# Scale and shift of the first norm folded into the query, key and value weights by another way, in a transformer block on one Trainium2 core

## The chip, the cores and the metric

One core of one Trainium2 chip. The metric is device time in microseconds for one launch. The kernel before takes 413.95 us, the median of three runs (413.38 to 415.32). A profiled execution of it took 416.01 us.

## What is computed

A block with adaptive layer norm: six modulation vectors come from a condition `c`; a linear attention with softmax feature maps; a feed-forward part with relu. x is 2048 x 576 in bf16, 32 heads of 18, feed-forward width 4608.

```python
mod = (silu(c) @ w_mod).reshape(1, 6, 1, 576)
sa, ca, ga, sb, cb, gb = ...                     # the six parts of mod
h = layernorm(x) * (1 + ca) + sa
q, k, v = split(h @ wqkv)                        # 32 heads of 18
pq, pk = q @ w_phi, k @ w_phi                    # per head
phi_q = concat(softmax(pq), softmax(-pq))        # 36 features; phi_k alike from pk
kv, z = phi_k^T v, sum over tokens of phi_k
o = (phi_q kv) / (phi_q z + 1e-6)
x = x + ga * (o @ wo)
h = layernorm(x) * (1 + cb) + sb
out = x + gb * (relu(h @ w1) @ w2)
```

## The kernel before

Tokens are in 16 tiles of 128 (t); two tiles are a unit or pair (u, p, n), four a block (b). The 576 features are five chunks of up to 128 (ci; the last has 64). The order of the work is one list of steps, written out by hand (line 922), that fixes the order on TensorE (PE), VectorE (DVE), ScalarE (ACT) and the DMA queue that SyncE (SP) issues; a step puts its instructions on the engines that it uses. An argument of 1 at the end of a copy's step picks the other engine (table at line 776: for most steps 0 is VectorE and 1 ScalarE; for KE, VE and QE 0 is ScalarE and 1 VectorE). GpSimd only clears tiles.

The scale 1 + ca and the shift sa are not applied to the tokens but to the weights. For keys (1) and queries (0) the weights are also multiplied by the feature map w_phi. The steps:

- Loads: LP, LP4 (x), LK (key and value weights, one chunk each, line 152), LA (first modulations, line 160), LH (w_phi, line 146), LQ (query weights, turned by the DMA, one group of six heads each, line 156), LM (other modulations), WOL, LW, W2 (weights of later parts).
- MC1 (line 307): products of the modulations, 25 matmuls of one column for each vector; MSC (316) and MSH (320) make 1 + ca (`mod[1]`) and sa (`sal`) of them. SIL makes silu(c).
- WT (331), WTE (337): TensorE turns one chunk of key weights, six transposes, and a copy brings them to `wT[1]`.
- F1, F0 (341): the turned weights times w_phi, six matmuls for a chunk. FA and FB (348) copy the two column halves from PSUM to `wplain`. SC1, SC0 (353) multiply `wplain` by the scale into `wfold`. SCv does so for the value weights.
- B1, B0, Bv (360): the shift times the weights, ten matmuls; BE (369) copies the two halves of that row into row 64 of the last chunk of `wfold` or `wv_sb`. The tokens carry a column of ones in that place.
- LS (line 220): mean and variance of one token tile; by VectorE (`bn_stats`) or ScalarE (two passes). RS (232): rstd. LX (236): normed tokens in bf16. PT and PX turn them on TensorE for units 0 and 1; LT (251) by DMA transposes for the other tiles. Z (200) is a matmul on zeros.
- K, V, Q (568): a projection of one tile, ten matmuls; KE, VE, QE its copy.
- For each block of keys MN and MX (least and greatest feature, 461), for each pair LO and HI (475), EX (exponential, 505), the sums, RC (527) and SC (533). Sums go either by SU (nine matmuls, 508) with SA (515), or by SD (one reduction on VectorE for each tile, 520). Here SD is used for tiles 12 and 13, which are pair 6. The q steps are the same for queries.
- KVa, KVb, KVc (616): products of keys and values over all tiles, 176 matmuls; KVE (629) brings them to SBUF. RW makes rows of modulations; WS (410) scales the output weights by a gate.
- Then NU, NUE, OT, OTE, WO, WOE, S2, R2, X2, PN, PNE for the first two tiles, and G, FW, RL, Y for their feed-forward part. From line 1020 on the other units run in a loop.

PSUM has a pool of three tiles of two banks (`mm`) and one of two single banks (`aux`). `room` is one stretch of SBUF that several tiles use one after another.

Of the kernel before, what the change touches and what calls it, by code (L numbers as in the profile page):

```python
# [8 lines left out]
P = 128  # L9
# [29 lines left out]
G6 = 6 * DH  # L39
VH = DH + 1  # L40
# [3 lines left out]
def kernel(  # L44
# [78 lines left out]
    wqT, wq_plain = part(3552, NGR, D), part(7008, KC, D)  # L123
# [10 lines left out]
    wT = {1: p0.tile([P, NGR, D], BF16, name="wT1"), 0: wqT}  # L134
    wplain = {1: part(0, KC, D), 0: wq_plain}
# [5 lines left out]
    A_.dma_start(crow[:], c)  # L141
    V.memset(wph[:, 5, :], 0.0)
# [9 lines left out]
    def load_keys_values(i):  # L152
        r = slice(i * P, i * P + KK[i])
        nc.sync.dma_start(kv_raw[0:KK[i], i, :], A_wqkv[r, D:3 * D])

    def load_turned(which, g):
        c0 = which * D + g * G6
        nc.sync.dma_start_transpose(out=wT[which][:, g, :], in_=A_wqkv[:, c0:c0 + P])
# [5 lines left out]
    V.memset(zeros[:], 0.0)  # L164
# [29 lines left out]
    zero_rows(wplain[1], wfold[1], wv_sb)  # L194
    for v in v_all:
        G.memset(v[:, :, :, DH:VH], 1.0)
    zero_rows(wplain[0], wfold[0])
# [7 lines left out]
    fill(1)  # L205
# [3 lines left out]
    spare = room[:, 9944:9944 + D]  # L209

    def norm_stats(t0, n, xn=None, how="V"):

        mv = work.tile([P, U, 2], FP32, name="mv", tag="mv", bufs=9)
        rs = work.tile([P, U], FP32, name="rstd", tag="rstd", bufs=9)
        if xn is None:
            xn = work.tile([P, U, KC * P], BF16, name="xn", tag="xn", bufs=2)

        by = {}

        def stats(j, eng=None):  # L220
            by[j] = how if eng is None else "VA"[eng is A_]
            junk = spare if eng is None else xn[:, j, 0:D]
            if by[j] == "V":
                st = work.tile([P, 2, 6], FP32, name="bst", tag="bst", bufs=4)
                for half in range(2):
                    V.bn_stats(out=st[:, half, :], in_=x_sb[:, t0 + j, half * 288:(half + 1) * 288])  # L226
                V.bn_aggr(out=mv[:, j, :], in_=st[:].rearrange("p a s -> p (a s)"))
            else:
                A_.activation(out=junk, in_=x_sb[:, t0 + j, :], func=ACT.Copy, scale=-1.0 / D, accum_out=mv[:, j, 0:1])
                A_.activation(out=junk, in_=x_sb[:, t0 + j, :], func=ACT.Square, bias=mv[:, j, 0:1], accum_out=mv[:, j, 1:2])  # L230

        def rstd():
            A_.activation(out=rs[:, 0:n], in_=mv[:, 0:n, 1], func=ACT.Ln, bias=eps_t[:], scale=1.0 if by[0] == "V" else 1.0 / D)
            A_.activation(out=rs[:, 0:n], in_=rs[:, 0:n], func=ACT.Exp, scale=-0.5)  # L234

        def norm():
            for j in range(n):
                V.tensor_scalar(out=xn[:, j, 0:D], in0=x_sb[:, t0 + j, :], scalar1=mv[:, j, 0:1],  # L238
                                scalar2=rs[:, j:j + 1], op0=ALU.subtract if by[j] == "V" else ALU.add, op1=ALU.mult)

        return xn, stats, rstd, norm

    hT1 = {}
    ln = [norm_stats(u * U, U, xn1[u % 3], how) for u, how in enumerate("VAVVAVAA")]
# [60 lines left out]
    mod, mod_ps = {}, {}  # L305

# [9 lines left out]
    def first_scale():  # L316
        mod[1] = const.tile([P, KC], FP32, name="mod1")
        V.tensor_scalar_add(mod[1][:], mod_ps[1, 1][:, 0:KC], 1.0)
# [12 lines left out]
    def fold_T(ci):  # L331

        ps = pool_tiles["T", ci] = mm_tile("ps_wT")[:, 0].bitcast(BF16)
# [7 lines left out]
    def fold(which, ci):  # L341
        ps = pool_tiles["F", which, ci] = mm_tile("ps_fold")
        for g in range(NGR):
            nf = G6 if g < 5 else 2 * DH
            T_.matmul(ps[0:KK[ci], g // 4, (g % 4) * G6:(g % 4) * G6 + nf], lhsT=wT[which][0:G6, g, ci * P:ci * P + KK[ci]],  # L345
                      rhs=wbd[0:G6, g, 0:nf], start=True, stop=True)

    def fold_out(which, ci, half, eng):
        ps, k = pool_tiles["F", which, ci], KK[ci]
        c0, n = ((0, 432), (432, 144))[half]  # L350
        copy(eng, wplain[which][0:k, ci, c0:c0 + n], ps[0:k, half, 0:n])
# [8 lines left out]
    def fold_bias(which, src):  # L360

        ps = pool_tiles["B", which] = mm_tile("ps_bias")
        for ci in range(KC):
            for half in range(2):
                p = 64 - half * 64
                T_.matmul(ps[p:p + 1, half, 0:288], lhsT=sal[:, ci:ci + 1], rhs=src[:, ci, half * 288:(half + 1) * 288],  # L366
                          start=(ci == 0), stop=(ci == KC - 1))

    def fold_bias_out(which, dst, half, eng):
        p = 64 - half * 64  # L370
        copy(eng, dst[64:65, 4, half * 288:(half + 1) * 288], pool_tiles["B", which][p:p + 1, half, 0:288])
# [196 lines left out]
    def project(name, t, w):  # L568
        b, j = t // TPB, t % TPB
        ps = pss[name, t] = mm_tile("ps_" + name)  # L570
        proj((ps[:, 0], ps[:, 1]), hT1[b][:, :, j * P:(j + 1) * P], w, HALVES if name == "v" else PARTS)

# [299 lines left out]
    def y(n, j, cols=HALVES):  # L872
# [7 lines left out]
        "RS": lambda u: ln[u][2](), "LX": lambda u: ln[u][3](), "LS": lambda t: ln[t // U][1](t % U), "LT": ln1_T,  # L880
# [10 lines left out]
        "SC1": lambda c, a=0: fold_scale(wfold[1], wplain[1], c, VA[a]), "SCv": lambda c, a=0: fold_scale(wv_sb, wv_raw, c, VA[a]),  # L891
        "SC0": lambda c, a=0: fold_scale(wfold[0], wplain[0], c, VA[a]),
        "B1": lambda: fold_bias(1, wplain[1]), "Bv": lambda: fold_bias("v", wv_raw), "B0": lambda: fold_bias(0, wplain[0]),
        "BE1": lambda h, a=0: fold_bias_out(1, wfold[1], h, VA[a]), "BEv": lambda h, a=0: fold_bias_out("v", wv_sb, h, VA[a]),
        "BE0": lambda h, a=0: fold_bias_out(0, wfold[0], h, VA[a]), "OPEN": open_p1, "PM": pad_keys, "LH": load_maps, "SD": lambda t: soft["K", t // TPB].sums(t % TPB),
        "K": lambda t: project("k", t, wfold[1]), "V": lambda t: project("v", t, wv_sb),
# [10 lines left out]
        "RC2": mod_columns, "Z": lambda k: fill(1), "MCE2": second_out, "RW": mod_rows,  # L907
# [142 lines left out]
```

## Time and profile before

| | |
|---|---|
| median of three runs | 413.95 us |
| the profiled execution's own time | 416.01 us |
| its span, first to last instruction | 414.1 us |
| TensorE busy | 406.1 us |
| VectorE busy | 235.2 us |
| ScalarE busy | 179.8 us |
| mean granted clock of TensorE | 0.996 |
| read from and written to HBM | 19.27 MB, 2.37 MB |

Busy time is the time in which an engine has at least one instruction under way. Each row of a timeline has the start and the length in us, the engine, the line, the operation, what is written from what, the number of instructions that were merged, and in brackets the idle time before it with what ended it. In the table by stretches each engine has its busy time with the number of instructions, and the granted clock stands behind the engines.

### The profile page before, as it was taken

To read this page: it belongs to the slowest core of one execution; us is meant where nothing else is said; L and a number is where in the kernel's file an instruction comes from. 1 tells how busy PE (TensorE), PEld (TensorE's weight loads), DVE (VectorE), ACT (ScalarE), POOL (GpSimd) and SP (SyncE) were. 2 spreads that over 40 slices of the span, in tenths; PEclk is the share of its full clock that TensorE was granted. 3 is DMA by queue.
4 is the path that set the end of the run, shared out by engine and by line. 5 is a ranking of instruction groups with operands and counts; after the bars stand their busy time and mean duration, and the time that the engine had idled before them with its cause. 6 is when DMAs were issued, how large, how long until landed. Compare 5 with 4: busy or idle time off the path is not lost.

```text
span 414.1 us, 9232 instructions
## 1 busy us (share of the span) xinstructions
PE 406.1 (98%) x3959; PEld 329.8 (80%) x3960; DVE 235.2 (57%) x600; ACT 179.8 (43%) x303; POOL 11.5 (3%) x37
## 2 busy tenths in 40 slices
PE   6899999999999999999999999999999999999997
PEld 4677777787887788788878888888888788888876
DVE  6879999999838565547446552846292532330011
ACT  6699999945761064016402630452055014302400
POOL 7100000000000000000000000000000000000000
PEclk9899999999999999999999999999999999999999
DMA  8957941399862620501051014104210501010001
GB/s 261 268 95 184 233 115 27 69 249 374 263 157 32 131 35 2 116 20 29 17 101 31 17 33 85 46 2 76 57 34 1 117 22 27 16 32 16 2 0 30
DMA packets 70978, 35.44 MB, mean 86 GB/s; under 512 B 56657, under 2 KB 67418, under 8 KB 70938
## 3 DMA queue, kind: packets, MB, share of 16 engines
q1 hardware_dynamic: 70336, 34.83, 35.1%
q8 instruction: 31, 0.51, 0.5%
q10 hardware_dynamic: 602, 0.02, 0.1%
q14 instruction: 9, 0.07, 0.0%
HBM read 19.27 MB, written 2.37 MB: 52 GB/s over the span
## 4 chain that ended last, share of the span: by engine, by line
PE 95%; DMA 3%; DVE 0%; ACT 0%; SPq 0%; issue 0%
PE ps_y L858 34%; PE ps_h L815 31%; PE ps_v L447 5%; PE ps_k L447 5%; PE ps_q L447 4%; PE ps_h L807 4%; PE ps_wo L723 3%; PE ps_sum L513 2%; DMA wma<-in_w_mod_dram 2%; PE ps_wo L447 2%; PE ps_kv L625 1%; DMA kv_raw<-in_A_wqkv_dram 1%; PE ps_num L666 1%; PE ps_bias L366 1%; PE ps_fold L345 0%; PE ps_row L381 0%
## 5 line engine op out<-in xcount | busy, mean ns | idle before, releaser
L820 ACT ACTIVATE H<-ps_h 128x1024 bf16<-128x1024 f32 x72 | 73.2, 1022 | 170.3 <-PE ps_h L807 121.5
L858 PE MATMUL ps_y<-w_sb,H 128*128 128x288 bf16 (+2 forms) x1188 | 143.0, 282 | 0.0
L858 PEld LDWEIGHTS <-H 128*128 128x128 bf16 x1188 | 113.7, 98 | 27.3
L815 PE MATMUL ps_h<-hT,w1a 128*128 128x256 bf16 x640 | 74.9, 273 | 0.4 <-DVE hT L418 0.4
L815 PEld LDWEIGHTS <-w1a 128*128 128x128 bf16 x640 | 61.2, 98 | 10.0 <-issue 2.8
L866 DVE TENSOR_TENSOR outt<-ps_y,row_gb 128x288 bf16<-128x288 f32 (+2 forms) x33 | 14.8, 448 | 84.0 <-PE ps_y L858 83.9
L815 PE MATMUL ps_h<-hT,w1b 128*128 128x256 bf16 x512 | 58.9, 273 | 0.0
L447 PEld LDWEIGHTS <-hT 128*128 128x128 bf16 x480 | 46.2, 98 | 13.0 <-ACT wv_sb L88 0.5
L815 PEld LDWEIGHTS <-w1b 128*128 128x128 bf16 x512 | 49.8, 98 | 6.6 <-issue 0.6
L728 DVE TENSOR_TENSOR x_sb<-x_sb,ps_wo 128x288 bf16<-128x288 bf16 x28 | 12.7, 454 | 32.5 <-PE ps_wo L723 24.8
L238 DVE TENSOR_SCALAR xn<-x_sb,mv,rstd 128x576 bf16<-128x576 bf16 x32 | 12.3, 425 | 21.6 <-ACT rstd L234 21.5
L447 PE MATMUL ps_v<-wv_sb,hT 128*128 128x288 bf16 x160 | 22.2, 291 | 0.0
L447 PE MATMUL ps_q<-wfold,hT 128*128 128x270 bf16 (+1 forms) x160 | 21.4, 285 | 0.0
L447 PE MATMUL ps_k<-wfold,hT 128*128 128x270 bf16 (+1 forms) x160 | 21.4, 285 | 0.0
L807 PE MATMUL ps_h<-hT,w1c 64*128 64x256 bf16 x288 | 19.9, 271 | 0.0
L506 ACT ACTIVATE room<-room 128x1188 bf16<-128x1188 bf16 x16 | 19.0, 1190 | 2.0 <-DVE room L479 1.5
L226 DVE BATCH_NORM_STATS2 bst<-x_sb 128x6 f32<-128x288 bf16 x46 | 18.5, 444 | 1.0 <-DMA x_sb<-in_A_x_dram 1.0
L524 DVE TENSOR_REDUCE ln_s<-room 128x66 f32<-128x1188 bf16 x14 | 19.0, 1365 | 0.0
L506 ACT ACTIVATE phik<-phik 128x2376 bf16<-128x2376 bf16 x8 | 17.4, 2184 | 0.0
L807 PEld LDWEIGHTS <-w1c 64*128 64x128 bf16 x288 | 12.1, 94 | 5.2 <-issue 3.8
L466 DVE TENSOR_TENSOR tree<-tree 128x264 bf16<-128x264 bf16 (+2 forms) x48 | 14.6, 304 | 1.6
L418 DVE TENSOR_SCALAR hT<-hT,mod 128x256 bf16<-128x256 bf16 x35 | 9.7, 342 | 8.2 <-DMA hT<-xn 8.2
(149 smaller groups left out, 362.0 us busy)
## 6 DMA issues: line engine op xcount, KB each, us to landing
w_sb<-in_B_w_dram SPq DMA_DIRECT2D x6, 864.0 KB, 7.4
out_dram<-outt SPq DMA_DIRECT2D x15, 144.0 KB, 1.8
w1b<-in_B_w_dram SPq DMA_DIRECT2D x2, 1024.0 KB, 9.6
x_sb<-in_A_x_dram SPq DMA_DIRECT2D x3, 576.0 KB, 7.3
w1a<-in_B_w_dram SPq DMA_DIRECT2D x2, 768.0 KB, 4.8
kv_raw<-in_A_wqkv_dram SPq DMA_DIRECT2D x4, 288.0 KB, 4.6
wma<-in_w_mod_dram SPq DMA_DIRECT2D x1, 1152.0 KB
wmb<-in_w_mod_dram SPq DMA_DIRECT2D x2, 576.0 KB, 4.3
```

Of the source, the lines that this page charges most:

```text
L226: V.bn_stats(out=st[:, half, :], in_=x_sb[:, t0 + j, half * 288:(half + 1) * 288])
L447: T_.matmul(ps[:, 0:cn], lhsT=lhs[:, ci, :], rhs=w[:, ci, cs:cs + cn], start=(ci == 0), stop=(ci == KC - 1))
L466: V.tensor_tensor(out=a[:, :, 0:w], in0=a[:, :, 0:w], in1=a[:, :, w:2 * w], op=op)
L506: A_.activation(out=E[:, j:j + k], in_=E[:, j:j + k], func=ACT.Exp)
L524: V.tensor_reduce(out=t["l", b][:, k * 22:(k + 1) * 22].rearrange("p (g s) h -> p g s h", s=2), op=ALU.add, axis=mybir.AxisListType.X, in_ ...
L723: T_.matmul(p[:, 0:cn], lhsT=oTs[n, j][:, ci, :], rhs=wo_sb[:, ci, cs:cs + cn], start=False, stop=(ci == 3))
L728: V.tensor_tensor(out=xs[:, cs:cs + cn], in0=xs[:, cs:cs + cn], in1=p[:, 0:cn], op=ALU.add)
L807: T_.matmul(f1[q][:, e, hh * w:hh * w + w], lhsT=w1["c"][r, 2 * q + hh, :], rhs=hT[r, 4, :], start=(first and hh == 0), stop=(not first an ...
L815: T_.matmul(f1[q][:, e, hh * w:hh * w + w], lhsT=w1_at(2 * q + hh, e, ci), rhs=hT[:, ci, :], start=(first and hh == 0 and ci == 0), stop=( ...
L820: A_.activation(out=p2t["H1"].rearrange("p (e j) n -> p e j n", e=2)[:, :, 2 * q:2 * q + 2], in_=f1[q][:].rearrange("p e (h n) -> p e h n" ...
L858: T_.matmul(ps[:, 0, 0:cn], lhsT=p2t["H1"][:, k, j * P:(j + 1) * P], rhs=p2t["w2"][:, k, c], start=(k == 0), stop=(k == NJ - 1))
L866: V.tensor_tensor(out=o[:, c], in0=ps[:, 0, 0:cn], in1=rows["gb"][:, c], op=ALU.mult)
```

## The change

Four things are changed, and the order of the steps is written anew.

1. `wplain` and the steps SC1 and SC0 are gone. FA and FB now multiply by the scale while they copy from PSUM to `wfold`.
2. B1 and B0 with their four copies are gone. TB1 and TB0 (`turned_shift`) multiply the raw weights, group by group, by the shift: thirty matmuls of one column. TE1 and TE0 copy that to a column behind the 576 of the turned weights `wT`. The fold of the last chunk takes 65 columns of `wT` in place of 64, so that row 64 of the folded weights is the bias. For the queries the raw weights are loaded as well (LR), since the DMA turns them on their way. The value bias keeps its ten matmuls.
3. LA, the first modulations, stands behind the first load of x. WT and the biases use the `aux` pool of PSUM.
4. SU.5 and SA.5 are replaced by SD.10 and SD.11.

LSM stands for LS in the first four tiles, one of each unit by VectorE and one by ScalarE, with variances of one scale (two small instructions more on ScalarE). ZZ.n is n matmuls on zeros; fifteen of them stand at the front in place of nine spread out, the one ahead of the first transfers included in both. Some copies change engines.

```diff
-    wqT, wq_plain = part(3552, NGR, D), part(7008, KC, D)
+    wqT, wq_raw = part(3552, NGR, DT), part(3552 + NGR * DT, KC, DX)
...
-    fill(1)
+    fill(3)
...
     def fold_T(ci):
 
-        ps = pool_tiles["T", ci] = mm_tile("ps_wT")[:, 0].bitcast(BF16)
+        ps = pool_tiles["T", ci] = aux_tile("ps_wT", BF16)
...
     def fold(which, ci):
-        ps = pool_tiles["F", which, ci] = mm_tile("ps_fold")
+        ps, k = mm_tile("ps_fold"), KK[ci] + (ci == KC - 1)
+        pool_tiles["F", which, ci] = ps
         for g in range(NGR):
             nf = G6 if g < 5 else 2 * DH
-            T_.matmul(ps[0:KK[ci], g // 4, (g % 4) * G6:(g % 4) * G6 + nf], lhsT=wT[which][0:G6, g, ci * P:ci * P + KK[ci]],
+            T_.matmul(ps[0:k, g // 4, (g % 4) * G6:(g % 4) * G6 + nf], lhsT=wT[which][0:G6, g, ci * P:ci * P + k],
                       rhs=wbd[0:G6, g, 0:nf], start=True, stop=True)
 
     def fold_out(which, ci, half, eng):
-        ps, k = pool_tiles["F", which, ci], KK[ci]
+        ps, k = pool_tiles["F", which, ci], KK[ci] + (ci == KC - 1)
         c0, n = ((0, 432), (432, 144))[half]
-        copy(eng, wplain[which][0:k, ci, c0:c0 + n], ps[0:k, half, 0:n])
+        d, m = wfold[which][0:k, ci, c0:c0 + n], mod[1][0:k, ci:ci + 1]
+        if eng is A_:
+            A_.activation(out=d, in_=ps[0:k, half, 0:n], func=ACT.Identity, scale=m)
+        else:
+            V.tensor_scalar_mul(d, ps[0:k, half, 0:n], m)
+
+    def turned_shift(which):
+
+        ps = pool_tiles["S", which] = aux_tile("ps_sh")
+        for g in range(NGR):
+            for ci in range(KC):
+                T_.matmul(ps[0:G6, g:g + 1], lhsT=w_raw[which][:, ci, g * G6:(g + 1) * G6], rhs=sal[:, ci:ci + 1],
+                          start=(ci == 0), stop=(ci == KC - 1))
+
+    def turned_shift_out(which, eng):
+        copy(eng, wT[which][0:G6, :, D], pool_tiles["S", which][0:G6, 0:NGR])
```

The new order up to the first feed-forward group (G):

```
LP.1 ZZ.3 Z.24 LA ZZ.2 LK.1 ZZ.4 LSM.2 Z.22 LK.4 LP.0 LK.0 Z.8 LK.3 LK.2 SIL LH WBD MC1.0 MSH LSM.3.1 RS.1 MC1.1
MSC WT.1 SCv.4.1 LX.1 WTE.1.1 WT.4 PT.1 LP4.2 WTE.4 LSM.1 F1.1 LSM.0.1 FA1.1.1 WT.0 WT.3 PX.1.0 WTE.0 PX.1.1.1 F1.0
FB1.0.1 WTE.3 SCv.3 RS.0 FB1.1 FA1.0.1 WT.2 TB1 WTE.2 SCv.1 LP4.4 F1.3 FB1.3.1 TE1 LX.0 F1.2 Bv FA1.3.1 LS.4 LP4.6
FA1.2.1 F1.4 FB1.2.1 SCv.2 FA1.4.1 FB1.4.1 LQ.5 PT.0 PX.0.0.1 K.3 LS.6 SCv.0 PX.0.1 LQ.2 BEv.1.1 OPEN BEv.0 KE.3
PM.2 K.2 LS.8 KE.2 V.2 LS.5 LS.7 LQ.3 PM.0 RS.2 LS.12 VE.2.1 RS.3 LX.2 K.0 PM.1 KE.0.1 V.3 CR V.0 LS.10 VE.3 LQ.1
V.1 LQ.0 K.1 LS.9 LQ.4 VE.1 LT.5 RS.4 VE.0.1 LR KE.1 LT.4 F0.3 LS.11 LX.3 RS.5 FA0.3 K.5 LT.7 FB0.3.1 MN.0 F0.1
KE.5 FB0.1.1 V.5 LT.6 F0.2 FA0.1.1 LX.5 LX.4 VE.5 LO.0 FB0.2.1 LT.11 LT.10 K.4 LM.1 F0.0 FA0.2.1 TB0 LS.13 FA0.0
KE.4 TE0 K.7 FB0.0.1 LT.8 KE.7 LO.1 F0.4 K.6 FA0.4.1 RS.6 MX.0 FB0.4 HI.0 Q.2 KE.6 LS.14 Q.3 QE.2 MN.1 QE.3 Q.0
LS.15 Q.1 V.4 QE.0 LO.2 QE.1 MX.1 LT.9 VE.4 RS.7 HI.1 Q.7 qMX.0 EX.1 K.9 QE.7 K.8 SU.1 LX.7 KE.9 LO.3 LX.6 qMN.0
PM.3 SA.1 K.10 qLO.0 LM.0 KE.8 LT.14 EX.0 K.11 K.14 SU.0 qHI.0 LT.12 qMN.1 LT.15 KE.11 KE.10 V.14 KE.14 RC.1 LT.13
HI.2 qEX.1 K.13 qEX.0 VE.14 K.12 MN.2 SA.0 RC.0 MX.2 KE.13 HI.3 qSU.0 KE.12 LO.5 LO.4 HI.5 K.15 EX.2 V.13 KE.15
HI.4 MN.3 LM.2 MX.3 RW.0 VE.13 EX.4 RW.1 V.7 VE.7 LO.7 RWE.1.1 WOL RWE.0.1 SU.2 Q.8 qSA.0 W1 LW.2.0 HI.7 Q.14 SC.1
V.6 RD.2 EX.5 SA.2 LW.0.1 SC.0 QE.14 qRC.0 RC2.0 V.9 QE.8 V.10 VE.6 RD.1 EX.3 SD.10 Q.13 VE.9 RC2.2 RD.0 SU.4 V.12
LW.1.1 QE.13 RC.2 LO.6 HI.6 V.11 SD.11 SC.2 EX.6 SU.3 VE.11 SA.4 qSC.0 VE.12 V.15 Q.4 RC.5 VE.10 Q.12 RC.4 QE.4 V.8
VE.15 SD.13 Q.11 RC2.1 SA.3 SC.5 SD.12 SC.4 EX.7 VE.8 WS.0 SU.7 LW.0.0 RC.3 SC.3 LW.1.0 SA.7 RC.6 KVa RC.7 QE.11
SC.6 qT.0 KVb SC.7 QE.12 MCE2 KVc WS.1 KVE.0.1 qMX.1 KVE.1.1 Q.10 NU.1 QE.10 NUE.1 Q.6 QE.6 NU.0 OT.1 NUE.0 OTE.1
Q.5 OT.0 WO.1 qHI.1 OTE.0 qLO.1 WOE.1 WO.0 WOE.0 qEX.2 Q.15 S2.0 S2.1.1 R2.1 Q.9 LW.2.1 X2.1 PN.1 R2.0 P2 W2.1.0
X2.0 PN.0 LW.3.0 W2.1.1 QE.5 QE.9 PNE QE.15.1 G.0 FW.2 ...
```

100 lines of the change are left out of this document (50 added, 50 removed).

## The prediction

> **What bounds the kernel now.** I read the page first, for the busiest engine and the chain that ended last.
>
> ```profile
> span 414.1 us, 9232 instructions
> PE 406.1 (98%) x3959; PEld 329.8 (80%) x3960; DVE 235.2 (57%) x600; ACT 179.8 (43%) x303; POOL 11.5 (3%) x37
> PE 95%; DMA 3%; DVE 0%; ACT 0%; SPq 0%; issue 0%
> ```
>
> TensorE is busy for 98% of the span and makes up 95% of the chain. So a change can help in two ways only: less TensorE work, or an earlier begin of the dense part. It can hurt by a wait put into that dense part. The table by stretches shows where the dense part is.
>
> ```profile
> 0.00:5.00 5.00, 2.92 (x10) 0.87 (x10) 2.85 (x13) 2.50 (x4) 4.11 (x17) 1.00 0.65 160
> 5.00:10.00 5.00, 3.97 (x30) 3.28 (x30) 3.39 (x11) 3.43 (x11) 4.14 (x8) 1.00 1.01 353
> 10.00:15.00 5.00, 3.56 (x75) 3.19 (x74) 3.96 (x12) 3.47 (x11) 0.00 (x0) 1.00 1.03 364
> ...
> 13.20:16.60 3.40, 2.49 (x65) 2.07 (x67) 2.24 (x8) 1.76 (x4) 0.33 (x2) 1.00 1.23 260
> 16.60:20.05 3.45, 3.45 (x26) 1.80 (x23) 3.42 (x12) 2.52 (x6) 1.32 (x8) 0.51 1.42 260
> ...
> 18.80:88.40 69.60, 69.60 (x714) 54.79 (x713) 65.07 (x139) 63.33 (x136) 1.76 (x6) 0.99 0.60 130
> 88.40:102.80 14.40, 13.93 (x169) 11.04 (x166) 12.53 (x34) 7.39 (x22) 0.00 (x0) 1.00 1.03 334
> ```
>
> The columns after the stretch are TensorE, weight load, VectorE, ScalarE, GpSimd, then the granted clock, the DMA share and GB/s. From 18.8 to 88.4 us TensorE never pauses, but VectorE is busy 65.07 of 69.60 us and ScalarE 63.33. These are two engines close behind the first: time taken from TensorE here is only won if VectorE follows. The chain of waits, in order of time, gives the begin and the prices.
>
> ```profile
> 6.00 8.29 DMA wma<-in_w_mod_dram
> 14.35 0.68 PE ps_mod L313 x21
> ...
> 15.61 0.62 PE ps_mod L313 x25
> ...
> 16.48 2.41 PE ps_bias L366 x20
> 18.89 4.37 PE ps_v L447 x30
> ...
> 29.66 0.38 PE ps_fold L345 x6
> ...
> 38.31 0.71 PE ps_bias L366 x10
> ...
> 44.12 3.68 PE ps_q L447 x30
> 47.80 1.19 PE ps_sum L513 x9
> ```
>
> The first 18.9 us run over transfers, the modulations last (landed at 14.3 us), then two bias products, and only then V.1.
>
> **TensorE work.** The query bias B0 goes: ten matmuls, 0.71 us (38.31). Pair 5's sums SU.5 go: nine matmuls, 1.19 us (47.80 shows such a set). TB0 comes in: thirty one-column matmuls; 25 such took 0.62 (15.61), so 0.74. The 65th row of the last fold adds no column to any matmul, so nothing. Net -0.71 - 1.19 + 0.74 = **-1.16 us**, all behind the start of the dense part. B1 and TB1 lie before it and count there.
>
> **The start.** Loads are issued on one queue. Before, the modulations are the eighth and ninth transfers and land at 14.3 us. After, they are second and third, and the last block of key and value weights, LK.2, is ninth, behind the same 3.24 MB. I take its landing at 13.4, between 11.8 (0.8 MB by 5 us at 160 GB/s, the other 2.44 at some 358) and 14.3 (the old ninth transfer). What must follow it is short now.
>
> ```profile
> 9.68 1.26 DVE L90 COPY wT<-ps_wT 108x768 bf16<-108x768 bf16 x2 [1.09 <-PE ps_wT L335]
> ...
> 9.84 0.50 PE L335 MATMUL ps_wT<-ident,kv_raw 128*108 128x128 bf16 x6
> ...
> 10.64 2.34 ACT L88 ACTIVATE room<-ps_fold 128x432 bf16<-128x432 f32 x7 [0.28 <-PE ps_fold L345]
> ```
>
> WT.2 on TensorE 0.5; its copy 0.63 beside TB1 (0.74); two folds 0.4 each with TE1 hidden; then ScalarE's last four to six copies from PSUM at 2.34/7 = 0.33 each, some 1.7 with the gaps; PT.0 lies beside them. 13.4 + 0.5 + 0.7 + 0.8 + 1.7 and 0.4 of hand-over is 17.5 us for K.3, against 18.89 for V.1. That the scale rides on the copy I cost at nothing: the pass reads the same PSUM columns. Bounds: nothing, and 0.39 each (the SBUF pass of line 358, 8 of which are below); the five on ScalarE beside TensorE's folds would put at most 1 us on the start, and I take nothing because the copy is nearest.
>
> The clock belongs to this sum. In the table it falls to 0.51 at 16.6 and is full at 20.05. V.1's thirty matmuls took 4.37, while thirty later ones took 3.68 (44.12), so 0.69 was lost and the effective start was 18.89 + 0.69 = 19.58. The stretch 13.2 to 16.6, which precedes the fall, is 2.49 of 3.40 us busy, but 50 matmuls of one column lie around it. After, the fills are moved to the first 8 us, and the stretch before K.3 holds transposes, folds and one-column TB1. I expect the same fall. Then K.3 runs at half rate from 17.5 to 20.05, loses 1.28, and the effective start is 18.78: **-0.8 us**. With a full clock it is 17.5: -2.1.
>
> The Trainium skill, "TensorE: Matmul & The Clock Gate", section "What's actually happening", says that an idle window of about 3.4 us halves the clock and that a busy one releases it. The trace agrees on the length, 3.45 us at 0.51. By that rule the front-loaded fills are spent before they matter, and the sum is the one with -0.8; if the new order's folds count as busy, it is the one with -2.1.
>
> **VectorE up to the last product of keys and values.** KVc needs SC.7, the last scaling.
>
> ```profile
> DVE xn L238 <- ACT rstd L234: 2.0, 1, 2.0
> ...
> 50.52 0.43 DVE L464 TENSOR_TENSOR tree<-pq 128x528 bf16<-128x528 bf16 x1
> ...
> 52.02 0.43 DVE L517 TENSOR_REDUCE ln_s<-ps_sum 128x132 f32<-128x264 f32 x1
> ...
> L524 DVE TENSOR_REDUCE ln_s<-phik 128x66 f32<-128x1188 bf16 x2 | 2.7, 1376 | 0.0
> L358 DVE TENSOR_SCALAR wfold<-room,mod 128x576 bf16<-128x576 bf16 x8 | 2.8, 385 | 0.0
> L90 DVE CAST phik<-ps_k 128x540 bf16<-128x540 f32 x3 | 2.1, 715 | 0.3 <-PE ps_k L447 0.3
> ...
> 84.44 3.99 DVE L537 TENSOR_TENSOR phik<-phik,rsum 128x2376 bf16<-128x2376 bf16 x3
> 88.36 1.05 DVE L412 TENSOR_TENSOR wo_sb<-wo_sb,row_ga 128x1728 bf16<-128x1728 bf16 x1
> ...
> 90.21 0.75 DVE L412 TENSOR_TENSOR wo_sb<-wo_sb,row_ga 128x1152 bf16<-128x1152 bf16 x1
> ```
>
> SC.7 ends at 88.36. KVc's 22 products are the last eighth of the chain's 5.08 us at 84.56, so they begin at 84.56 + 154/176 x 5.08 = 89.0; the slack is 0.6.
>
> ```profile
> 84.56 5.08 PE ps_kv L625 x176
> 89.66 0.64 DVE KVZ L639
> ...
> 90.52 0.81 ACT KVZ L637 x4
> ```
>
> Ahead of SC.7 VectorE gains: two sums SD at 1.34 (2.7), the root qMN.1 (50.52 to 52.02, 1.5), WS.0 (0.75), one copy of values (0.7), small ones (0.5): +6.1. It loses: SC0 four passes at 0.32 to 0.39 (1.4), four copies of keys and queries that go to ScalarE (0.73 with the small one: 2.9), one sum from PSUM (0.35): -4.7. Net +1.4. Of the 4.5 us in which it wasn't busy before, 2.0 is the wait for ScalarE's rstd, some 1.0 are three small ones, and 1.5 lies between instructions. So from K.3 on it has 65.1 + 1.5 + 1.4 = 68.0 us to do, and with 1.8 us of waiting it ends at 17.5 + 68.0 + 1.8 = 87.3. TensorE reaches KVc at 18.78 + (89.0 - 19.58) - 1.16 + 1.23, since Q.11 now runs ahead of the products: 88.3. VectorE has 1.0 us to spare, little over the old 0.6, and its waits are a guess: **+0.3**, with bounds 0 and 2. ScalarE gains four copies and loses six passes or bias rows; it comes out even.
>
> **Behind the products.** Q.11 covered KVZ before; Q.10 does now. KVE.0 moves to ScalarE, so its three instructions and the five of KVE.1 stand in one line: at 0.25 and 0.2 some 1.75, against 89.66 to 91.33, 1.67. One Q fewer covers the chain from NU.1 to G.0: **+0.15**, bounds 0 and 0.6. From 102.8 on nothing is moved that TensorE waits for.
>
> Two waits are new in the dense part. TB0 needs the raw query weights of LR.
>
> ```profile
> wmb<-in_w_mod_dram SPq DMA_DIRECT2D x2, 576.0 KB, 4.3
> ```
>
> LR has that size and goes out behind LT.5, which left at 25.4 before; at 4.3 us it is there by 31, and TB0 stands three projections and four folds behind F0.3, at 33.5 by the sum of rival 3 below. F0.4 needs the 65th column from TE0, with K.7 (1.23) in between. Both at nothing; if the cover fails, K.7 and all behind it on TensorE waits, by as much as LR is late beyond these 2.5 us.
>
> Sum: -1.16 - 0.8 + 0.3 + 0.15 = **-1.5 us**. The profiled execution took 416.01 against its span of 414.10, and the runs have a median of 413.95; the difference is carried over as it is: 412.4 for the median, and 412.6 for a span.
>
> **Rivals.** (1) The clock is full at K.3. For it: the fold stretch holds more real matmuls, and 10 to 15 us before was full with such. Effective start -2.1, TensorE at KVc 87.0, VectorE 0.3 late: 413.95 - 1.16 - 2.1 + 0.3 + 0.15 = 411.1.
>
> (2) VectorE becomes the bound. Every microsecond that it waits beyond 2.8 is TensorE's. Half as much again as the old 3.0 us, 4.5, leaves KVc 1.7 late: 412.4 - 0.3 + 1.7 = 413.8. For it: the last table row but one, 65.07 of 69.60. Against it: most of its work there has no other engine's result to wait for at the last moment, 1.0 us of small waits.
>
> (3) The turned query weights, on the other side. F0.3 needs all six of them and it stands right after eight projections; K.5 and all else on TensorE is queued behind it.
>
> ```profile
> 13.68 0.58 SPq L102 DMA_DIRECT2D x_sb<-in_A_x_dram  x1
> 14.31 6.74 SPq L158 DMA_TRANSPOSE room<-in_A_wqkv_dram  x4
> ...
> 28.00 0.43 PE L345 MATMUL ps_fold<-room 108*128 108x108 bf16 x6
> ...
> L158 SPq DMA_TRANSPOSE room<-in_A_wqkv_dram x6: 1239/1506/4690, 7.7 to 19.3; - x6
> ...
> DMA to landing us min/median/max: 5.5/8.5/9.8
> ```
>
> Before, two of the six are issued ahead of the last x load and the sixth at 19.3, for a fold at 28.0. After, all six stand behind every x load, and F0.3 comes at 18.78 + 8 x 1.23 = 28.6. If they go out only once the loads are through, at 1.69 each from 14.0, the sixth leaves at 22.5 and lands at 31.0 by the median (2.4 late, 414.8) or 32.3 by the slowest (3.7 late, 416.1). It decides from an issue later than 20.1. Against it: the queue may be free from 7.6 on. LT.5, LR and LT.4 are behind the same six.
>
> (4) The change doesn't do what it says: LK.2 lands like the old ninth transfer and ScalarE's line of copies is longer, K.3 at 18.9, half rate to 20.05: effective 19.5, so 413.1.
>
> **Chances.** About 0.5% (2.07 us) is what a measurement of this kernel can tell from no change: faster is below 411.9, slower above 416.0. Forecast 0.38, with its own range 411.6 to 413.4; rival 1 0.22; rival 2 0.10; rival 3 0.18; rival 4 0.12. Faster: rival 1 and a third of the forecast, 0.34. Slower: the slow end of rival 3, and its middle where rival 2 or 4 comes on top, 0.17. Same: 0.49. The range 410.8 to 415.8 leaves out the slow end of rival 3 and an early landing with full clock.
>
> **What would show it.** K.3 at 17.0 to 18.0 and a half clock ending near 20; no TensorE wait at F0.3 nor at K.5; a ps_bias row less, a ps_sum set less; SC.7 ending within 0.6 us of KVc; four sums on line 524's kind of instruction in the keys. A wait of TensorE on VectorE at ps_kv would be rival 2, on a DMA into room rival 3. The prediction fails if LK.2 lands after 14.5, or if TensorE shows more than 1 us of waits between 20 and 100 us.

## The result, and the profile after

The changed kernel takes 417.65 us (median of 6 runs, 417.5 to 419.45) against 413.87 us before (6 runs, 413.38 to 415.32): a ratio of 1.0097, interval 1.0073 to 1.0121. It is slower, by 3.8 us. The forecast was 412.4 us, with a range of 410.8 to 415.8.

The page of the changed kernel, the same three lines as before: span, busy time, and the chain by engine.

```profile
span 415.5 us, 9290 instructions
PE 407.3 (98%) x3997; PEld 332.2 (80%) x3997; DVE 233.7 (56%) x587; ACT 182.3 (44%) x311; POOL 11.1 (3%) x37
PE 96%; DMA 3%; DVE 0%; ACT 0%; issue 0%
```

TensorE is still the bound, but it is busy for 1.2 us more than before, although the change takes work from it; some 6.8 us of the span ran at half clock, against 3.4 in the profile before (granted clock 0.992 and 0.996). The chain of the changed kernel (start, length, what) tells where.

```profile
3.87 7.56 DMA wph<-in_A_w_phi_dram
11.45 0.89 DVE room L287 x3
12.55 0.08 DVE mod L328
12.62 1.50 PE ps_wT L345 x12
...
17.97 1.45 PE ps_sh L373 x30
...
21.63 2.49 PE ps_k L473 x20
...
36.22 1.49 PE ps_sh L373 x30
...
87.05 5.08 PE ps_kv L661 x176
...
92.44 1.55 ACT KVZ L673 x7
```

The dense part begins with K.3 at 21.63 us; 17.5 was forecast. The chain into it is one that no part of the prediction names. The small load of w_phi (`LH`) lands at 11.43. Then VectorE makes the block-diagonal form of it (`WBD`, line 287). Only behind that, in VectorE's fixed order, come the shift and the scale (`MSH`, and `MSC`, line 328). From 12.62 to K.3 the chain is TensorE's own work without a wait. The waits of the three engines (engine, waiting tile and line, releaser: total us, times, longest):

```profile
PE ps_wT L345 <- DVE mod L328: 3.1, 1, 3.1
...
PE ps_mod L323 <- DMA wma<-in_w_mod_dram: 0.4, 1, 0.4
PE ps_h L851 <- DVE hT L444: 0.4, 1, 0.4
```

```profile
DVE room L287 <- DMA wph<-in_A_w_phi_dram: 4.3, 1, 4.3
ACT wv_sb L382 <- DVE mod L328: 5.3, 1, 5.3
```

So one late transfer of 20 KB stands ahead of all three: VectorE 4.3 us, TensorE 3.1, ScalarE 5.3. TensorE is held because WT now uses the `aux` pool: its two buffers still hold the modulations' products until `MSH` and `MSC` have read them. No run here gives WT its old pool back. Before, the same operation (line 279 there; VectorE's work in order of time) waited for nothing:

```profile
7.23 0.89 DVE L279 TENSOR_TENSOR room<-wph,m_hd 108x270 bf16<-108x270 bf16 x3
```

The table by stretches of the changed kernel, with the columns of the prediction's table (TensorE, weight load, VectorE, ScalarE, GpSimd, clock, DMA share, GB/s), shows the second half of the loss.

```profile
7.00:10.20 3.20, 2.12 (x53) 1.55 (x51) 0.17 (x1) 0.28 (x2) 2.22 (x5) 1.00 1.06 289
10.20:12.60 2.40, 0.00 (x0) 0.01 (x1) 1.15 (x8) 0.00 (x0) 0.00 (x0) 0.57 1.09 352
12.60:17.20 4.60, 4.56 (x43) 4.39 (x44) 3.11 (x10) 4.31 (x9) 0.00 (x0) 0.50 1.06 377
17.20:21.60 4.40, 4.40 (x82) 3.97 (x81) 3.80 (x13) 3.13 (x9) 0.00 (x0) 0.98 1.16 157
```

While TensorE stands idle, the clock falls to half, and then the transposes and folds from 12.6 to 17.2 run at 0.50. In finer windows the half clock lasts from 10.55 to 17.38. The forecast had a half clock too, but half as long and later, from 16.6 to 20.05.

From K.3 on the total of the forecast holds: 415.5 - 21.63 = 393.87 us. The prediction has 412.6 - 18.78 = 393.82. Its terms don't all hold, though (see the account of the prediction below).

### The profile page after: what moved, and what is told of

The parts are those of the page before. It is cut to its first block, busy times and chain, and to the rows that moved or that the text cites. A ratio compares the mean times of both kernels' runs of the same rounds, so it can differ in the third digit from the quotient of the medians.

```text
span 415.5 us, 9290 instructions
## 1 busy us (share of the span) xinstructions
PE 407.3 (98%) x3997; PEld 332.2 (80%) x3997; DVE 233.7 (56%) x587; ACT 182.3 (44%) x311; POOL 11.1 (3%) x37
## 4 chain that ended last, share of the span: by engine, by line
PE 96%; DMA 3%; DVE 0%; ACT 0%; issue 0%
PE ps_y L894 34%; PE ps_h L851 31%; PE ps_v L473 5%; PE ps_k L473 5%; PE ps_q L473 4%; PE ps_h L843 4%; PE ps_wo L759 3%; PE ps_sum L539 2%; DMA wph<-in_A_w_phi_dram 2%; PE ps_wo L473 2%; PE ps_kv L661 1%; PE ps_num L702 1%; PE ps_fold L356 1%; PE ps_wT L345 1%; DMA x_sb<-in_A_x_dram 1%; PE ps_sh L373 1%
## 5 line engine op out<-in xcount | busy, mean ns | idle before, releaser
L902 DVE TENSOR_TENSOR outt<-ps_y,row_gb 128x288 bf16<-128x288 f32 (+2 forms) x33 | 14.7, 446 | 87.5 <-PE ps_y L894 87.5
L764 DVE TENSOR_TENSOR x_sb<-x_sb,ps_wo 128x288 bf16<-128x288 bf16 x28 | 12.6, 452 | 33.4 <-PE ps_wo L759 24.8
L532 ACT ACTIVATE phik<-phik 128x2376 bf16<-128x2376 bf16 x8 | 17.5, 2193 | 0.2 <-DVE phik L505 0.2
```

The source lines that it names most:

```text
L532: A_.activation(out=E[:, j:j + k], in_=E[:, j:j + k], func=ACT.Exp)
L764: V.tensor_tensor(out=xs[:, cs:cs + cn], in0=xs[:, cs:cs + cn], in1=p[:, 0:cn], op=ALU.add)
L902: V.tensor_tensor(out=o[:, c], in0=ps[:, 0, 0:cn], in1=rows["gb"][:, c], op=ALU.mult)
```

## What the experiments tell apart

Each kernel was timed beside the kernel before on the same chip (414.40, 414.37 and 414.16 us in the three groups); the ratios are against that one. The changed kernel itself was not timed again in these groups, so differences from its 417.65 are between groups. K.3 and V.1 are given from the chain, as 21.63 is; a timeline has them 0.1 to 0.2 us earlier, because there an instruction overlaps the one before it.

**Theory A**: `WBD` holds VectorE up because the load of w_phi is issued too late, behind `SIL` on ScalarE's queue; issued first, K.3 is back near the forecast. **Rival B**: with the modulations first, the key and value weights come too late whatever VectorE does. **Rival C**: the loss sits in the dense part behind K.3, where VectorE could be the bound behind pair 5's sums.

**maps_first**: `LH` is the first step.

```
-LP.1 ZZ.3 Z.24 LA ...    SIL LH WBD MC1.0
+LH LP.1 ZZ.3 Z.24 LA ... SIL WBD MC1.0
```

> The changed kernel with one step moved: LH (the load of w_phi) is the first step, so that ScalarE's queue issues it at about 1.3 us in place of 3.9 us. Theory A: WBD stands ahead of MSH and MSC on VectorE, waits there for w_phi (4.3 us), TensorE then waits 3.1 us for the scale and falls to half clock from 10.2 to 17.2 us. By A the wait is gone, MSC ends at about 9.8 us, K.3 starts at 16.5 to 18.6 us in place of 21.6, and the time falls from 417.65 by 3 to 5 us, to 412.7 to 414.7. Rival B: loading the modulations first brings the key and value weights too late whatever VectorE does; K.3 stays at 20.5 us or later and the time above 416.5. Rival C: the loss sits in the dense part behind K.3; the time stays within 1 us of 417.65.

Measured: 417.29 us (ratio 1.0066, interval 1.0045 to 1.0086); K.3 at 21.84. Of the two rows the first is ScalarE's issue, the second VectorE's use of what it loaded.

```profile
1.31 0.34 ACTq L149 DMA_DIRECT2D wph<-in_A_w_phi_dram  x1
```

```profile
10.62 0.90 DVE L287 TENSOR_TENSOR room<-wph,m_hd 108x270 bf16<-108x270 bf16 x3 [3.44 <-DMA wph<-in_A_w_phi_dram]
```

Issued 2.6 us earlier, the load is there only 0.8 us earlier: it takes over 9 us to land. It is many tiny pieces (602 packets, 0.02 MB) beside the modulations' 1.33 MB, which in this order are on their way from the start. Theory A in its simple form falls: the late issue is not the cause by itself. TensorE still waits 2.3 us for the scale. Rival B's numbers are met, but TensorE waits for no weights, so B stays open here.

The table of this run shows something of the clock besides.

```profile
11.40:14.80 3.40, 3.01 (x30) 3.04 (x31) 2.50 (x13) 2.82 (x6) 0.00 (x0) 0.51 0.94 319
14.80:18.20 3.40, 3.08 (x61) 2.94 (x59) 2.64 (x8) 2.77 (x8) 0.00 (x0) 0.99 1.35 320
18.20:21.55 3.35, 3.35 (x35) 2.43 (x33) 3.14 (x11) 2.21 (x6) 0.00 (x0) 0.50 0.87 175
```

It opens behind a stretch that is mostly transposes, and falls again behind one in which TensorE was busy for 3.08 of 3.40 us.

**maps_late_wbd_behind_scale**: `LH` stays late, `WBD` goes behind `MSC` (`WBD MC1.0 ... MSC WT.1` becomes `MC1.0 ... MSC WBD WT.1`).

> The changed kernel with WBD moved behind MSC in the order, and LH left where it is, so w_phi still lands at about 11.4 us. It tells the block on VectorE apart from the late landing itself. If the block is what costs: MSH and MSC at 9.7 us, WT.1 at about 9.8 us in place of 12.6, TensorE waits at most for F1.1 at 12.3 us, K.3 at 18.0 to 19.5 us, time 414 to 416. If the late landing costs as much by itself, because F1.1 can't start without the maps: K.3 at 20.5 us or later, time above 416.5.

Measured: 419.88 us (1.0114, interval 1.0082 to 1.0146), K.3 at 24.38 in the profiled execution. The executions differ: two at a clock of 0.992 took 416.73 and 417.70, the four at 0.983 to 0.988 took 419.6 to 420.8. The profiled one is of the latter. The waits of TensorE:

```profile
PE psT_h L270 <- DVE xn L246: 2.8, 1, 2.8
```

The block only moved on, to the first x values that VectorE turns behind `WBD`. The half clock lasted from 11.3 to 24.9.

**wbd_just_before_fold**: `LH` first, and `WBD` right before F1.1, its first reader. **Theory A2**: the modulations, ahead in the DMA engines, slow the small packets of w_phi, and the loss is TensorE's idle gap behind `WBD` with the half clock that follows it.

> The changed kernel with LH as the first step and WBD moved from ahead of MSH to just before F1.1, its first reader. The first four runs showed that w_phi lands at 10.2 us even if it is issued at 1.3 us, and that either place of WBD so far stopped VectorE and then TensorE for 2.3 to 3.6 us. Theory A2: the modulations' 1.33 MB, ahead in the DMA engines, slow the 602 small packets of w_phi; the loss is the idle gap of TensorE behind WBD, and the half clock that follows it. By A2 no wait of TensorE above 1 us is left after 9.5 us, K.3 starts at 18.0 to 19.5 us, time 413.5 to 415.5. Rival B: the weights LK.0, LK.3, LK.2, which the queue issues late behind the modulations, set K.3; it stays at 20.5 us or later and the time at 416.5 or more.

Measured: 419.62 us (1.0114, interval 1.0093 to 1.0135), K.3 at 23.11. TensorE's waits are down to 1.0 and 0.7 us:

```profile
PE ps_fold L356 <- DVE room L287: 1.0, 1, 1.0
PE ps_mod L323 <- DMA wma<-in_w_mod_dram: 0.7, 1, 0.7
```

and the kernel is 2 us slower than the changed one that waits 3.1. Its table by stretches, same columns:

```profile
7.00:10.60 3.60, 2.83 (x64) 2.20 (x63) 1.21 (x7) 0.36 (x1) 2.20 (x5) 0.96 1.05 267
10.60:14.00 3.40, 2.40 (x24) 2.23 (x23) 2.59 (x9) 3.09 (x8) 0.00 (x0) 0.50 0.99 340
14.00:17.40 3.40, 3.39 (x35) 3.19 (x35) 2.51 (x6) 2.14 (x6) 0.00 (x0) 0.50 1.13 376
17.40:20.80 3.40, 3.40 (x39) 2.97 (x40) 1.58 (x6) 1.11 (x3) 0.00 (x0) 0.50 1.20 166
20.80:24.00 3.20, 3.20 (x27) 2.37 (x24) 1.61 (x7) 2.28 (x6) 0.93 (x7) 0.50 0.55 95
```

Four windows at 0.50, two of them with TensorE busy for 3.39 and 3.40 of 3.40 us. The busy share isn't what opens the clock: in these windows TensorE does transposes, folds and thirty products of one column (2.91 us at half rate). The Trainium skill, "TensorE: Matmul & The Clock Gate", section "Part 4: PE-mode transpose", says that transposes don't count as busy for the gate in the same way. These windows agree, and show that this mix with folds and one-column products didn't open it either. Other windows don't fit so well: in maps_first the clock opened at 14.7 and in the changed kernel at 17.4, each time behind transposes and folds. Which part of the mix decides is open. A2's account of the loss falls: the wait is nearly gone and the kernel is slower. So there is a **theory D**: the clock, not the wait alone, sets the start.

**mods_load_third**: as the last, with the modulations loaded behind the first two blocks of weights.

> As the first kernel of this set, but with LA behind LK.1 and LK.4 in the load queue. By A2 the small packets of w_phi get 0.44 MB of other loads beside them and not 1.33 MB, land at 5 to 7 us, and WBD waits for nothing; the modulations land about 1.2 us later, near 9.5 us, so MSC is at 10.5 to 11 us. TensorE then idles for the modulations instead. Time 413.5 to 416, no better than the first kernel by more than 1 us. If the small packets are late for another reason, they land at 10 us again and the time is that of the first kernel or above.

Measured: 421.19 us (1.0139, interval 1.0105 to 1.0174): a miss. TensorE now waits 3.5 us for the modulations (`wma`, line 323), the clock is half from 9.2 to 26.2, and K.3 comes at 25.73. Two executions at a clock of 0.992 took 418.2 and 418.6, the other four 420.9 to 422.6.

One half of A2 is shown here. In the trace's record of packets the last one of w_phi ends at 4.6 us; in wbd_just_before_fold, where only the modulations' place in the queue differs, it ends at 10.1, and in the kernel before at 4.3. So it is the modulations loaded first that make w_phi late, more than its own late issue.

**before_with_mods_load_first**: the kernel before with `LA` behind its first x load, nothing else.

> The kernel before with one load moved: LA (modulations) behind the first x load instead of behind the last key and value weights; nothing else. By A2 w_phi, issued at 1.3 us as always, lands near 10 us in place of 4.7 us, WBD holds up VectorE, V.1 starts 2 to 4 us later and the time rises from 413.9 to 416 to 419. Rival: the modulations were the last load that the start waited for, so that loading them first gains up to 1 us even here: 412.5 to 414.

Measured: 417.26 us (1.0054, interval 1.0035 to 1.0073), V.1 at 20.59. The amount is as expected; the way is another. TensorE's waits and chain:

```profile
PE ps_wT L335 <- DMA kv_raw<-in_A_wqkv_dram: 4.7, 1, 4.7
```

```profile
2.87 6.85 DMA kv_raw<-in_A_wqkv_dram
9.77 2.20 PE ps_wT L335 x18
...
20.59 3.78 PE ps_v L447 x30
```

Here it is the weights that come late, since the modulations travel ahead of them. W_phi is late too (its last packet ends at 9.7 us), but `WBD` doesn't wait for it: VectorE had waited 5.5 us for x before. So in the old order the part "modulations loaded first" by itself moves the start of the dense part back by 2.9 us.

**before_spans**: the kernel before once more, to see how its profiled executions differ.

> The kernel before, run again, for the span and granted clock that go with its times. The profiled execution took 416.01 us with a span of 414.10, while the median is 413.9. If the distance of time and span is a constant 1.9 to 2.1 us, as it is in the changed kernel (417.61 and 415.5), usual runs of the kernel before have spans of about 411.9 and a granted clock above 0.996, and its profiled execution was one with a longer stretch of half clock. If not, the spans are 414 and only the overhead varies.

Measured: 414.32 us, ratio 0.999, interval 0.9971 to 1.001. Its chain and its table around the start:

```profile
6.14 8.01 DMA wma<-in_w_mod_dram
...
16.32 1.37 PE ps_bias L366 x20
17.70 3.78 PE ps_v L447 x30
...
36.54 0.71 PE ps_bias L366 x10
```

```profile
13.00:16.40 3.40, 3.02 (x78) 2.63 (x77) 2.79 (x10) 2.27 (x6) 0.29 (x2) 1.00 1.19 287
16.40:19.80 3.40, 3.40 (x38) 2.46 (x35) 3.37 (x13) 2.90 (x7) 1.17 (x8) 1.00 1.46 263
```

Span 412.3 us, time 414.25, no half clock. The execution that the prediction was worked out from (416.01) had one window at 0.51 that most executions of this kernel don't have. Of 17 in one group, five show a mean clock of 0.996 and took 415.6 to 416.7 us; the others, at 1.0 or 0.999, took 413.6 to 414.7. One half-rate window costs some 1.8 us, and the usual effective start before is 17.8, not 19.58.

**pair5_on_pe**: pair 5's sums back on TensorE (`SD.10 SD.11` become `SU.5 SA.5`).

> The changed kernel with pair 5's sums back on TensorE (SU.5 in place of SD.10, SA.5 in place of SD.11). Theory A and the prediction's term: nine matmuls come back to an engine without waits, so the time rises by 1.2 us to 418.8. Rival: VectorE, which has 2.3 us less to do, was the hidden bound between K.3 and the products; the time falls or stays at 417.65.

Measured: 419.48 us (1.0118, interval 1.0095 to 1.0141), 1.8 more than the changed kernel. That figure is between groups, and from only four runs. The profile is plainer: K.3 is at 22.16, and from there to the end of the span it is 395.0 us against 393.87, so the nine products cost 1.2. The move to VectorE gains what was forecast. Rival C falls, here and in the other runs: from K.3 to the end it is 393.9 us in maps_first too, and 393.9 and 393.8 in the two runs with fills below that change only the start.

**shift_on_128_columns**: the turned shift reads 128 columns of the raw weights in place of 108 (the rows beyond 108 of its result are not used).

```
-T_.matmul(ps[0:G6, g:g + 1], lhsT=w_raw[which][:, ci, g * G6:(g + 1) * G6],
+T_.matmul(ps[:, g:g + 1], lhsT=w_raw[which][:, ci, g * G6:g * G6 + P],
```

> The changed kernel with the weight loads of TB1 and TB0 128 columns wide in place of 108 (the 20 columns more give rows that nobody reads). In the changed kernel a load of 108 columns takes 130 ns and the thirty matmuls 1.49 us, while the modulations' 128-column loads take 96 ns and 25 matmuls 0.62 us. If the width of the load is the reason: 0.75 us for each set, and 417.65 falls by 0.75 (TB0) to 1.5 us (both), to 416.2 to 416.9. If it is not: 1.45 to 1.5 us each and no change in time.

Measured: 416.35 us (1.0045, interval 1.003 to 1.006), 1.3 less than the changed kernel. The profiled execution, at 417.68, is the slowest of the eleven; what it shows is the length of the loads. The weight loads of line 373 (min/median/max ns), first in the changed kernel, then here:

```profile
L373 PEld LDWEIGHTS <-room x30: 128/130/130, 36.0 to 37.5; 128*108 128x108 bf16 x30
```

```profile
L373 PEld LDWEIGHTS <-room x30: 95/96/98, 36.8 to 37.5; 128*128 128x128 bf16 x30
```

```profile
36.96 0.73 PE ps_sh L373 x30
```

A product of one column goes at the pace of its weight load: with 108 columns the load takes 130 ns and the thirty products 1.49 us, with 128 columns 96 ns and 0.73 us. TB0 as forecast would have been this second form. The Trainium skill, "TensorE: Matmul & The Clock Gate", section "Weight-path perf modes — Fast Weight Load (FWL) and DoubleRow", says that the fast load is on only for 128 weights not in FP32; the two rows agree.

**Theory D**, tried by filling. `ZM.n` is n products of 512 columns on zeros, whose result is not used, put into TensorE's line where it waits.

**fills_in_the_gap**: the changed kernel with three ahead of MC1.0 and ten between MC1.1 and WT.1.

```
-SIL LH WBD MC1.0 MSH LSM.3.1 RS.1 MC1.1 MSC WT.1
+SIL LH WBD ZM.3 MC1.0 MSH LSM.3.1 RS.1 MC1.1 ZM.10 MSC WT.1
```

> The changed kernel with thirteen matmuls on zeros more: three ahead of MC1.0 and ten between MC1.1 and WT.1, in a PSUM tile of the other pool; every wait stays as it is. Theory A2 has fallen: with WBD out of the way TensorE waited 1.0 us only and the kernel was slower still, 419.6, at half clock from 10.7 to 24.0 us. Theory D: the loss is the clock gate; between 7.5 and 12.6 us TensorE does only one-column matmuls or nothing, the gate closes, and the folds that follow run at half rate. By D the fills keep it open, the 9.0 us from WT.1 to K.3 become 6.5 to 7.5, K.3 starts at 19 to 20 us, granted clock 0.996 or more, time 415 to 416.3. Rival E: the waits and the late weights set K.3, the clock only fills them; no gain, 417.3 to 418.

Measured: 416.65 us (1.0053, interval 1.0037 to 1.0069), K.3 at 20.18. Its table over the stretch that was at half clock, and TensorE's work in order of time (the bracket is the wait ahead of it):

```profile
12.60:20.10 7.50, 6.89 (x121) 6.16 (x122) 6.70 (x21) 7.16 (x18) 0.00 (x0) 1.00 1.14 276
```

```profile
9.03 2.32 PE L210 MATMUL ps_warm<-zeros 128*128 128x512 bf16 x10
...
12.57 0.85 PE L350 MATMUL ps_wT<-ident,kv_raw 128*108 128x128 bf16 x12 [1.22 <-DVE mod L333]
...
20.02 2.64 PE L478 MATMUL ps_k<-wfold,hT 128*128 128x270 bf16 x20
```

Full clock, and K.3 1.45 us earlier, though TensorE still begins WT.1 at 12.57. The clock alone is worth 1.0 us by the medians, 1.3 if each is taken against the kernel before of its own group. By the numbers of its expectation this is neither D (at most 416.3) nor E (at least 417.3), but between them: the clock is a part of the loss, the rest is still there. Two of eleven executions had a clock of 0.996 even so.

**fills_and_no_block**: `LH` first, `WBD` behind LX.1, and fills of 3, 4, 4 and 2 along the way.

```
-SIL LH WBD MC1.0 MSH ... MC1.1 MSC WT.1 SCv.4.1 LX.1 WTE.1.1 WT.4 PT.1 ... WT.0 WT.3 ...
+SIL ZM.3 MC1.0 MSH ... MC1.1 ZM.4 MSC WT.1 SCv.4.1 LX.1 WBD WTE.1.1 WT.4 PT.1 ZM.4 ... WT.0 WT.3 ZM.2 ...
```

> As the kernel with thirteen fills in the gap, but with LH first, WBD behind LX.1 and the thirteen fills spread (three ahead of MC1.0, four behind MC1.1, four behind PT.1, two behind WT.3). By D, with the gate open, it is now that the removed block of VectorE shows: K.3 at 17.5 to 19 us, clock 0.997 or more, time 413 to 414.8. By E: K.3 at 21 us or later, 417 or more.

Measured: 414.79 us (1.0015, interval 0.9998 to 1.0032), K.3 at 19.06, clock 1.0 in the profiled execution. Three of twelve had 0.996 and took 416.2 to 416.5, the others 414.4 to 415.1: the same kernel, some 1.7 us apart by the clock. Much the same removal of the block that cost 2.0 us without fills (419.62 against 417.65) gains 1.9 with them. Here `WBD` stands a few steps earlier, and the fills are spread otherwise.

**fills_no_block_128_columns**: the last two edits together with the 128-column shift.

> As the kernel with fills and no block, with TB1 and TB0 on weight loads of 128 columns, which alone brought 417.65 to 416.35. By D 0.75 to 1.4 us less than that kernel: 412 to 413.8, at or below the kernel before. By E the same as the loads of 128 columns alone, 416 or more.

Measured: 413.75 us (0.9984, interval 0.9969 to 0.9999). The fastest version: level with the kernel before, or some 0.6 us ahead of it. From its chain:

```profile
9.80 0.89 PE ps_warm L210 x4
10.68 0.67 PE ps_wT L350 x12
...
11.91 0.86 PE ps_warm L210 x4
...
15.02 0.73 PE ps_sh L378 x30
...
17.95 2.49 PE ps_k L478 x20
```

So the changed kernel's time goes 417.65, 416.65, 414.79, 413.75: clock 1.0, block 1.9, weight loads 1.0. By the spans of the profiled executions (415.5, 414.1, 412.9, 411.2) it is 1.4, 1.2 and 1.7, so each of the three is worth 1 to 2 us. TensorE waits for no load between 2 us and the end here, in the same order of transfers as in maps_first, so rival B falls as well.

K.3 at 17.95 is no earlier than V.1 at 17.70 before. Even with these three put right, the new start gains nothing; what is gained lies in the dense part. But the thirteen fills themselves now stand in the chain, 2.85 us of it. Whether some could go without the clock falling was not tried.

**before_four_fills_less**: the kernel before without Z.23, Z.8, Z.11 and Z.3.

> The kernel before without the four matmuls on zeros that stand between its folds and modulations (Z.23, Z.8, Z.11, Z.3), some 0.2 to 0.4 us each and mostly in idle time. By D they are what keeps the gate open there: without them the clock falls for a window or two in most runs, granted clock 0.996 or less, time 415 to 417.5. Rival: they do nothing, and the time is that of the kernel before, 413.9 to 414.4, or 0.5 less.

Measured: 416.23 us (1.0032, interval 1.001 to 1.0054). Its executions at a mean clock of 0.992 took 416.6 to 416.9 us and those at 0.996 took 415.8 to 416.3; at 1.0 most took 413.6 to 414.5. That is six of twelve below 0.999, against five of 34 of the kernel before beside it. So four fills fewer bring the half clock back in many executions of the old order too. Two at a clock of 1.0 took 416.83 and 417.65; what delayed these is open.

## Why the prediction was wrong, point by point

**The start: wrong, and here lies most of the miss.** The step that failed is "13.4 + 0.5 + 0.7 + 0.8 + 1.7 and 0.4 of hand-over is 17.5 us for K.3". Its first term held: LK.2 was issued at 8.2 and landed 4.6 us later, at 12.8. But the sum takes the other blocks to be turned and folded by then, and they weren't. WT.1, the first of them, began only at 12.62. From there to K.3 are 9.0 us of TensorE's own work, some 6.6 at full clock, where the sum has 4.1.

What held WT.1 up is the load of w_phi, for which the sum has no term. The working prices what `LA`'s move to the front does to LK.2, but not what it does to `LH`. The new order has `WBD`, which needs that load, ahead of MSH and MSC in VectorE's line, and so ahead of WT.1. K.3 came at 21.63 in place of 17.5. Neither of the two signs of failure that the prediction names came up: LK.2 was there before 14.5, and TensorE didn't wait between 20 and 100 us.

**The clock: the right mechanism in the wrong place, and half its size.** The forecast put one half-rate window over K.3 itself, from 17.5 to 20.05, for 1.28 us. In the profile after, there are two, from 10.55 to 17.38, on the way to K.3; from 12.62 on, where TensorE has work, that is 4.8 us at half rate, or some 2.4 lost, of which the fills won back 1.45. The clock is full when K.3 runs. That the fills at the front are spent before they matter held, and it decides more than the forecast gave it: 1.0 to 1.4 us here, 4.8 between the kernel with little waiting and no added fills, 419.62, and the one with fills, 414.79 (in that pair `WBD` also stands a few steps apart).

**The effective start**, then: 18.78 forecast, 21.63 measured, 2.85 late. The span's miss is 415.5 - 412.6 = 2.9.

**From span to median: wrong.** "The difference is carried over as it is" made a span of 412.6 into 412.4. The median after lies 2.15 us above its profiled span, in the kernel before (412.3 to 414.32) some 2.0. The profiled execution of before was one with an extra half window, so its effective start of 19.58 was 1.8 us later than usual. That is 2.35 us of the miss; with the 2.85 and 0.05 elsewhere it makes the 5.25 between 412.4 and 417.65. Told another way: against the usual start, 17.8, the forecast's own 18.78 was a loss of 1.0, not a gain of 0.8.

**TensorE work: one term of three mis-sized.** B0 went (0.71); pair 5's sums are worth about the 1.19; TB0 took 1.49 in place of 0.74, because the row taken for it (25 such in 0.62) has loads of 128 columns. Net -0.41, not -1.16. TB1, in the start, was mis-sized in the same way. The scale on the copy, put at nothing, made ScalarE's copies of 432 columns 616 ns long in place of 538; the chain doesn't run over them.

**VectorE: mis-sized in the other direction.** SC.7's end and KVc's begin decide, from VectorE's work in order of time:

```profile
88.49 2.69 DVE L563 TENSOR_TENSOR phik<-phik,rsum 128x2376 bf16<-128x2376 bf16 x2
...
91.10 0.16 DVE L337 TENSOR_SCALAR mod<-mod 128x5 f32<-128x5 f32 x1
```

The two scalings end at 91.2, and KVc's 22 products begin at 87.05 + 154/176 x 5.08 = 91.5. That leaves 0.3 us to spare, less than the forecast's 1.0, and no wait of TensorE at ps_kv: nothing in place of 0.3. Rival 2 did not occur; VectorE kept up with TensorE from K.3 on.

**Behind the products**: from the end of the last product to G.0 it is 12.28 us with five Qs (92.13 to 104.41), before 13.15 with six (87.87 to 101.02); less one Q of 1.23, that is +0.36 for a forecast of +0.15. Inside its bounds.

**Rival 3 did not occur**: no TensorE wait at F0.3 nor at K.5, nor any between 20 and 100 us. The last of the turned query weights was issued at 19.2 us, ahead of the 20.1 from which it was to decide. **Rival 1** (full clock at K.3) held as to the clock, but with K.3 4.1 us later it is not the case that was priced. **Rival 4** is the nearest: the start no earlier. It doubted the start, but for another cause (LK.2 and ScalarE's copies), and by 0.7 us of effective start in place of 2.85.

The dense part as a whole, against the usual before: 393.87 - (412.3 - 17.8) = -0.6, with -0.7 forecast. The terms as measured, -0.41, 0 and +0.36, make only -0.05. About 0.2 of the rest lies behind G.0 (311.09 us from there to the end, 311.28 before); the remaining 0.4 is not attributed. So the agreement of the dense part with the forecast is in part luck: what was mis-sized is made up by what wasn't in the sum.

## What to carry to other kernels

When a step is moved, follow every load it needs by its own row to the engine whose fixed order it stands in: here one of 20 KB, itself delayed by a large load moved ahead of it, held three engines for 3 to 5 us. Before a sum is made from one profiled execution, see whether its half-rate windows are usual, because one is worth as much as the whole change. And where a wait is removed from a stretch of transposes and short products, the clock may take the gain and more, as it did here (419.62 against 417.65 us); thirteen products of 512 columns decided the sign here.

## What the runs showed of the hardware that was not expected

- TensorE at 3.39 and 3.40 us busy of 3.40 stayed at a clock of 0.50 through two windows of transposes, folds and one-column products, the second of them followed by one more at 0.50 over K.3; in much the same order with thirteen products of 512 columns among them it was 1.00. In two other runs it opened behind transposes and folds, so the rule is not settled.
- A load of 20 KB in 602 packets took 7.56 us to land when issued at 3.87, and about 9 when issued at 1.31, beside 1.33 MB of modulations. With the modulations behind two blocks of weights its last packet ended at 4.6 us, with them first at 10.1, issued alike. By what part of the DMA path they hold it up was not separated.
- Thirty one-column products cost 1.49 us with weights of 108 columns and 0.73 with 128: fewer weights, twice the time.
- Executions of one and the same kernel differ by one half-rate window: five of 17 of the kernel before had it, and took 415.6 to 416.7 us in place of 413.6 to 414.7.
